# Windowed attention and softplus feed-forward: a new hand-written opening that reaches slot 9

## The chip, the cores and the metric

One NeuronCore of a Trainium2 chip runs the whole program. The metric is the time of one execution on the device in microseconds. Before the change the median of three runs is 897.19 us (895.76 to 897.30).

## The reference

```python
def _attn_ref(q, k, v):                       # q, k, v: (8, 8, 576, 64)
    scores = scale * np.matmul(q, k.transpose(0, 1, 3, 2))
    mask_plain = (rel >= 0) & (rel < 32)
    mask_dil = (rel >= 0) & (rel < 128) & (rel % 4 == 0)
    masks = ...                               # plain for heads 0 to 3, dilated for 4 to 7
    scores = np.where(masks, scores, -1e9)
    attn = softmax(scores)                    # sum + 1e-9 under the exponentials
    return np.matmul(attn, v)

x = attn_out.transpose(0, 2, 1, 3).reshape(4608, 512)
h = x @ w_in                                  # (512, 2048)
g = np.maximum(h, 0) + np.log1p(np.exp(-np.abs(h)))
return g @ w_out                              # (2048, 512)
```

## The kernel before

The 4608 tokens are cut into nine chunks of 512. A chunk has four attention groups of two heads each (groups 0 to 3 are chunk 0, 4 to 7 are chunk 1, and so on); the first two groups of a chunk have the plain window, the last two the dilated one. Only keys in the window are multiplied, in blocks of 32 queries by 64 keys. The feed-forward has 16 slices of 128 hidden columns (ff). Every product is made of three matrix products, from a high and a low part of each factor: high by high, high by low, low by high.

The first two chunks run through 32 *slots*, one for a chunk and a slice each, listed by `RUNS`: slots 0 to 5 are slices 0 to 5 of chunk 0, slots 6 to 15 slices 0 to 9 of chunk 1, slots 16 to 25 the rest of chunk 0, slots 26 to 31 the rest of chunk 1. Slot i has four H parts (`h_part(i, kt)`, line 545: hidden columns from the 128 input columns kt, which are those of attention group kt of the chunk) and four O parts (`o_part(i, m)`, line 610: output columns m). O of slot i - 2 follows H of slot i. An O part adds into its output bank over the slots of a run; at the last slot of the run the four banks are copied to SBUF and sent to DRAM (`kept_part`, line 637), to be added when the chunk resumes.

Weights arrive as 64-bit words and are decoded on the chip, one tensor (ff, 0 for w_in or 1 for w_out) in seven steps (`decode_step`, line 141): D0 absolute value (ScalarE), D1 to D4 clamp, shift and merge (VectorE), D5 the high part (ScalarE), Dl the low part (VectorE, or GpSimd for the first five).

All of the work up to a certain place is written out by hand in the string `OPENING` (line 71). Each word is one step; the instructions of an engine run in the order of the words. The words are: k, q, v, m, r loads of keys, queries, values, masks and raw weights (r0, r1, ... in the order in which slots need them: (0,0), (1,0), (0,1), (2,0), (1,1), (3,0), ...); S the scores of a group, M their maximum, E the exponentials (16 rows on ScalarE), Z the divisor, P the division (GpSimd; Pv on VectorE), T four transposes on TensorE, C the copy of their result (ScalarE; Cv on VectorE), V the product with the values, Xh and Xl the high and low part of its result; H and O the parts of a slot; A the three activation rows on ScalarE, G the softplus sum, Gh and Gl its high and low part; F that many filler products on zeros, whose result is not read. The list before ends with O of slot 4 (`OPENED = 6`); from slot 7 on a loop (line 917) writes H and O parts in turn and puts the other work between them by planned times.

PSUM is laid out by tags: "h" with two banks for hidden columns, "att" with two banks, "o0" to "o3" for the output parts. Scores of odd groups of chunk 0 use the two h banks, all other scores use att. Transposes use o0 and value products o1 and o2 for chunk 0, and att for every later group:

```python
self.turned_to = two_banks("t_ps", ("o0",) if self.own else None)[0][0]    # transposes, own: chunk 0
banks, src = two_banks("a_ps", ("o1", "o2") if self.own else None)         # weighted
```

Of the kernel before, what the change touches and what calls it, by code (L numbers as in the profile page):

```python
# [39 lines left out]
NKT = DM // P  # L40
NPR = H // 2
NFF = DF // P
RUNS = ((0, 6), (1, 10), (0, 10), (1, 6))
OPENED = 6
FIRST = 2
HALF = CH // 2
NPAIR = NFF // 2
# [4 lines left out]
LAG = 2  # L52
# [16 lines left out]


OPENING = """
k0 q0 m0 k1 q1 v0 F8 S0 q2 M0 k2 F1 S1 q3 E0 M1 r0 k3 E1 F7 S2 Z0 P0 r1 M2 F2 T0 v1 D0_0_0 Z1 S3
P1 E2 C0 v3 V0 M3 r2 T1 D1_0_0 Xh0 D2_0_0 E3 v2 C1 Xl0 m1 D3_0_0 F5 V1 r3 Z2 D4_0_0 Xh1 P2 k5 Xl1
D0_0_1 q4 Z3 F6 T2 D5_0_0 P3 k4 D0_1_0 q5 C2 D1_1_0 D1_0_1 v4 F4 V2 D2_0_1 D3_0_1 T3 k6 Xh2 D4_0_1
S4 C3 Xl2 Dl0_0 r4 D5_0_1 Dl0_1 M4 F1 H0_0 D0_2_0 r5 V3 D2_1_0 E4 D3_1_0 H0_1 r6 D4_1_0 H0_2 Xh3
D1_2_0 Xl3 v5 D2_2_0 F3 H0_3 D5_1_0 D3_2_0 S5 q6 A0 Z4 Dl1_0 r7 M5 P4 H1_0 D0_3_0 H1_1 G0 r8 E5
H1_2 Gh0 Gl0 H1_3 k7 D1_3_0 D2_3_0 D3_3_0 r9 A1 F3 T4 Z5 D4_2_0 D4_3_0 r10 G1 P5 C4 D5_2_0 F7 V4
r11 D0_1_1 Gh1 Gl1 D5_3_0 D1_1_1 Xh4 v6 Dl3_0 Xl4 Dl2_0 D0_3_1 q7 F7 T5 r12 D2_1_1 D0_2_1 H2_0
D3_1_1 C5 H2_1 D4_1_1 r13 H2_2 D1_2_1 D5_1_1 V5 D2_2_1 D3_2_1 r14 D4_2_1 H2_3 Xh5 D1_3_1 O0_0
D5_2_1 Xl5 Dl1_1 A2 O0_1 v7 S7 Dl2_1 r15 D2_3_1 D0_4_0 O0_2 G2 D0_5_0 O0_3 M7 r16 H3_0 D1_4_0 H3_1  # L80
E7 D2_4_0 r17 H3_2 D3_4_0 H3_3 D4_4_0 O1_0 Gh2 r18 Gl2 D5_4_0 O1_1 Z7 A3 S6 Dl4_0 r19 D1_5_0 O1_2
D2_5_0 D0_4_1 M6 P7 O1_3 r20 H4_0 G3 E6 H4_1 D3_5_0 r21 H4_2 D4_5_0 H4_3 D3_3_1 O2_0 r22 D5_5_0
Gh3 T7 Z6 A4 Dl5_0 O2_1 Gl3 r23 O2_2 D4_3_1 O2_3 C7 G4 P6 H5_0 r24 D5_3_1 H5_1 D0_6_0 Gh4 V7 Gl4
r25 Dl3_1 H5_2 Xh7 D1_4_1 H5_3 D0_5_1 Xl7 r26 O3_0 A5 D2_4_1 T6 D3_4_1 O3_1 r27 D4_4_1 O3_2 C6
D1_6_0 G5 O3_3 r28 D5_4_1 Gh5 V6 Gl5 Dl4_1 H6_0 Xh6 r29 D1_5_1 H6_1 D0_7_0 Xl6 D2_5_1 H6_2 r30
D2_6_0 H6_3 D3_6_0 O4_0 D4_6_0 A6 r31 O4_1 D3_5_1 O4_2 D4_5_1 D5_6_0 O4_3 D1_7_0 G6 D5_5_1 Gh6 Gl6
Dl5_1 Dl6_0 D2_7_0 D3_7_0 D4_7_0 D5_7_0 Dl7_0
"""


# [1 line left out]
def tile_windowed_attention_softplus_ffn(  # L92
# [201 lines left out]
    class Group:  # L294
# [7 lines left out]
        def __init__(self, c, pr):  # L302
            self.c, self.pr, self.dil = c, pr, pr >= NPR // 2
            self.own, self.masked = c == 0, c < 2

        def load_k(self, engine=None):
            kw = DKW if self.dil else PKW
# [92 lines left out]
            ))  # L400

        def transposes(self):
            self.turned_to = two_banks("t_ps", ("o0",) if self.own else None)[0][0]
            for m in range(NS):
                tc.keep_in_program_order(
                    nc.tensor.transpose(
                        out=self.turned_to[:, m * P : (m + 1) * P],
                        in_=self.s[:, m * P : (m + 1) * P],
                        identity=ident,
                    )  # L410
                )
            self.pt = scratch([P, CH], "pt", self.c, self.pr)
# [36 lines left out]

        def weighted(self):  # L450

            banks, src = two_banks("a_ps", ("o1", "o2") if self.own else None)
            for i in range(NB):
                t2, g = divmod(i, NG)
                for h in range(2):
                    for r in range(2):
                        rows = slice(r * D, (r + 1) * D)
                        if self.dil:
                            at = g * (PER // 2) + t2 * BLK
                            dst = banks[h][rows, at : at + BLK]  # L460
                        else:
                            by_class = banks[h][rows, :HALF].rearrange("p (r i) -> p r i", r=DIL)
                            dst = by_class[:, :, i * BLK // DIL : (i + 1) * BLK // DIL]
                        matmul(
                            out=dst,
                            lhsT=self.v[h * WKEYS : (h + 1) * WKEYS, i, r, :],
                            rhs=self.weights_of(h, r * 2 + t2, g),
                            start=True,
                            stop=True,
                        )  # L470
            if self.c >= FIRST:
                self.x = x_half(self.c, self.pr // 2)[:, self.pr % 2], None, src
# [50 lines left out]
    def at(when, part, *what, cost=0.0):  # L523
        heapq.heappush(events, (when, next(serial), cost, part, what))
# [128 lines left out]
    def fillers(n):  # L653
# [523 lines left out]
```

## Time and profile before

| | before |
|---|---|
| median of 3 runs | 897.19 us |
| the profiled execution | 896.0 us |
| its span, first to last instruction | 893.9 us |
| TensorE busy | 873.5 us, 98% |
| VectorE busy | 607.5 us, 68% |
| ScalarE busy | 551.2 us, 62% |
| GpSimd busy | 49.0 us, 5% |
| granted TensorE clock, mean | 0.99 |

Busy shares are means over the whole span. The page cuts the span in 40 slices of 22.3 us: TensorE is busy 6, 9 and 8 tenths of the first three, the granted clock is 8 tenths in the first two, and GpSimd works in the first three alone. In the chain that ended last TensorE has 89% of the span, VectorE 4%, ScalarE 3%, DMA and its queue 2%. Times in the views count from the start of the span.

### The profile page before, as it was taken

To read this page: it belongs to the slowest core of one execution; us is meant where nothing else is said; L and a number is where in the kernel's file an instruction comes from. 1 tells how busy PE (TensorE), PEld (TensorE's weight loads), DVE (VectorE), ACT (ScalarE), POOL (GpSimd) and SP (SyncE) were. 2 spreads that over 40 slices of the span, in tenths; PEclk is the share of its full clock that TensorE was granted. 3 is DMA by queue.
4 is the path that set the end of the run, shared out by engine and by line. 5 is a ranking of instruction groups with operands and counts; after the bars stand their busy time and mean duration, and the time that the engine had idled before them with its cause. 6 is when DMAs were issued, how large, how long until landed. Compare 5 with 4: busy or idle time off the path is not lost.

```text
span 893.9 us, 22746 instructions
## 1 busy us (share of the span) xinstructions
PE 873.5 (98%) x9186; PEld 747.8 (84%) x9186; DVE 607.5 (68%) x1216; ACT 551.2 (62%) x1355; POOL 49.0 (5%) x47
## 2 busy tenths in 40 slices
PE   6989899999999999999999999999999999999998
PEld 3668678888888888888888888888888888899997
DVE  2799889898678667655765666667666766565544
ACT  4676687766756566556665565557555765455443
POOL 1320000000000000000000000000000000000000
PEclk8899999999999999999999999999999999999999
DMA  9778222764465456554555455544654564334333
GB/s 345 285 256 330 73 75 74 273 234 147 156 208 172 151 157 209 173 166 148 196 191 167 145 178 206 163 156 165 194 171 159 160 204 135 106 106 154 95 95 118
DMA packets 84296, 154.12 MB, mean 172 GB/s; under 512 B 9312, under 2 KB 25824, under 8 KB 84192
## 3 DMA queue, kind: packets, MB, share of 16 engines
q1 hardware_dynamic: 83472, 151.49, 50.4%
q8 instruction: 73, 1.20, 0.6%
q10 hardware_dynamic: 720, 1.18, 0.4%
q14 instruction: 31, 0.25, 0.1%
HBM read 125.37 MB, written 27.26 MB: 171 GB/s over the span
## 4 chain that ended last, share of the span: by engine, by line
PE 89%; DVE 4%; ACT 3%; issue 1%; DMA 1%; SPq 1%; ACTq 0%; DVEq 0%
PE o_ps L182 42%; PE h_x L182 18%; PE h_y L182 14%; PE h_ps L182 7%; PE a_ps L182 4%; PE s_ps L182 3%; ACT s L377 1%; DVE a L166 1%; DMA k<-kpl 1%; DVE a L161 1%; DVE parts L176 1%; SPq L131 1%; ACT ob L638 0%; ACT parts L173 0%; DVE e L567 0%
## 5 line engine op out<-in xcount | busy, mean ns | idle before, releaser
L182 PE MATMUL o_ps<-gh,t 128*128 128x512 f32 (+1 forms) x904 | 341.2, 391 | 0.0
L182 PEld LDWEIGHTS o_ps<-gh,t 128*128 128x128 f32 x904 | 169.8, 188 | 21.3
L560 ACT ACTIVATE e<-hs 128x512 f32<-128x512 f32 x112 | 70.3, 627 | 188.0 <-DVE hs L956 188.0
L182 PE MATMUL o_ps<-gl,t 128*128 128x512 f32 (+1 forms) x452 | 178.4, 395 | 0.0
L582 ACT CAST gh<-e 128x512 fp32r<-128x512 f32 x137 | 84.6, 618 | 64.3 <-DVE e L567 63.4
L588 DVE TENSOR_TENSOR gl<-e,gh 128x512 fp32r<-128x512 f32 x144 | 104.2, 724 | 10.8 <-ACT gh L582 9.5
L182 PEld LDWEIGHTS h_x<-a,parts 128*128 128x128 f32 x672 | 95.2, 189 | 9.8 <-DVE hs L956 0.3
L182 PEld LDWEIGHTS h_y<-s,t 128*128 128x128 f32 x672 | 93.9, 188 | 9.0
L182 PE MATMUL h_y<-s,t 128*128 128x256 f32 x672 | 99.6, 284 | 0.0
L182 PE MATMUL h_x<-a,parts 128*128 128x256 f32 x672 | 98.1, 282 | 0.0
L562 ACT ACTIVATE e<-e 128x512 f32<-128x512 f32 x144 | 91.2, 633 | 4.6
L561 ACT ACTIVATE e<-e 128x512 f32<-128x512 f32 x144 | 91.1, 633 | 4.6
L956 DVE TENSOR_TENSOR hs<-h_x,temps 128x256 f32<-128x256 f32 x112 | 47.4, 423 | 66.2 <-PE h_x L182 64.8
L182 PE MATMUL o_ps<-gh,parts 128*128 128x512 f32 x256 | 88.9, 399 | 3.5 <-ACT ob L638 3.5
L956 DVE TENSOR_TENSOR temps<-h_y,temps 128x256 f32<-128x256 f32 x112 | 47.5, 424 | 61.2 <-PE h_y L182 61.1
L182 PEld LDWEIGHTS o_ps<-gl,t 128*128 128x128 f32 x452 | 86.4, 191 | 3.1 <-DVE gl L588 0.4
L182 PE MATMUL h_ps<-xh,parts 128*128 128x512 f32 x256 | 87.9, 399 | 0.0
L395 POOL TENSOR_TENSOR s<-s,ri 128x512 f32<-128x512 f32 x36 | 41.4, 1149 | 685.7 <-DVE ri L392 485.3
L567 DVE SCALAR_TENSOR_TENSOR e<-hs,e 128x512 f32<-128x512 f32 x112 | 76.3, 681 | 1.8 <-ACT e L562 1.8
L377 ACT ACTIVATE s<-s,nm 128x64 f32<-128x64 f32 x224 | 74.8, 336 | 3.9 <-DVE nm L369 3.9
L182 PEld LDWEIGHTS o_ps<-gh,parts 128*128 128x128 f32 x256 | 48.7, 190 | 14.1 <-ACT ob L638 3.9
L182 PEld LDWEIGHTS h_ps<-xh,parts 128*128 128x128 f32 x256 | 48.6, 190 | 10.4
(80 smaller groups left out, 1223.1 us busy)
## 6 DMA issues: line engine op xcount, KB each, us to landing
t<-w_out SPq DMA_DIRECT2D x224, 256.0 KB, 3.0
v<-vp SPq DMA_DIRECT2D x36, 512.0 KB, 4.1
raw<-w SPq DMA_DIRECT2D x32, 512.0 KB, 9.0
q<-qp SPq DMA_DIRECT2D x36, 256.0 KB, 3.2
w_out<-parts SPq DMA_DIRECT2D x16, 512.0 KB, 4.7
out_t<-ob SPq DMA_DIRECT2D x32, 256.0 KB, 2.3
turned<-squares SPq DMA_DIRECT2D x28, 256.0 KB, 3.6
pt<-turned SPq DMA_DIRECT2D x112, 64.0 KB, 2.8
```

The lines of the kernel that those rows point to most:

```text
L131: tc.keep_in_program_order((engine or nc.sync).dma_start(**kw))
L161: pin(nc.vector.scalar_tensor_tensor(out=ai, in0=low, scalar=29, in1=ai, op0=ALU.logical_shift_right, op1=ALU.bitwise_or,))
L182: tc.keep_in_program_order(nc.tensor.matmul(**kw))
L377: pin(nc.scalar.activation(out=self.blocks[:, t], in_=src, func=AF.Exp, bias=self.nm[:, t : t + 1], scale=1.0 / 8.0 if self.masked else 1. ...
L395: pin((engine or nc.gpsimd).tensor_tensor(out=self.blocks, in0=self.blocks, in1=self.ri.unsqueeze(2).to_broadcast([P, NB, WKEYS]), op=ALU. ...
L560: pin(nc.scalar.activation(out=e, in_=tiles[i], func=AF.Abs))
L561: pin(nc.scalar.activation(out=e, in_=e, func=AF.Exp, scale=-1.0))
L562: pin(nc.scalar.activation(out=e, in_=e, func=AF.Ln, bias=1.0))
L567: pin(nc.vector.scalar_tensor_tensor(out=e, in0=tiles.pop(i), scalar=0.0, in1=e, op0=ALU.max, op1=ALU.add))
L582: pin(nc.scalar.copy(out=gh, in_=ready[i]))
L588: pin(nc.vector.tensor_tensor(out=gl, in0=e, in1=gh.bitcast(F32), op=ALU.subtract))
L956: pin(nc.vector.tensor_tensor(out=dst, in0=src, in1=temps[:, temp], op=ALU.add))
```

## The change

It rewrites `OPENING`, which now goes on to O of slot 7 (`OPENED = 9`), and moves the start of chunk 2's attention in the planned part from 9 to 10.2 slots. Groups 4 and 5 get the banks o0 (transposes) and o1, o2 (value products) that chunk 0's groups have, through `AHEAD = 6`. An output bank is taken by its own O part and no longer by part 0 for all four. The four copies after slot 5 are words of the list (K). The high part of g is on VectorE for slots 0 to 9, but for slot 4 (Gs, ScalarE); after slot 9 it is on ScalarE. One division (Pv4) and two copies (Cv4, Cv7) are on VectorE. There are 38 fillers in place of 54.

```diff
-OPENED = 6
+OPENED = 9
+AHEAD = 6
 OPENING = """
-k0 q0 m0 k1 q1 v0 F8 S0 q2 M0 k2 F1 S1 q3 E0 M1 r0 k3 E1 F7 S2 Z0 P0 r1 M2 F2 T0 v1 D0_0_0 Z1 S3
...
+k0 q0 m0 k1 q1 q2 v0 F9 S0 k2 M0 r0 E0 F3 S1 r1 M1 k3 Z0 E1 q3 F5 S2 P0 v1 M2 T0 k4 D0_0_0 Z1 v2 C0
...
@@ class Group
             self.own, self.masked = c == 0, c < 2
+            self.ahead = c * NPR + pr < AHEAD
...
-            self.turned_to = two_banks("t_ps", ("o0",) if self.own else None)[0][0]
+            self.turned_to = two_banks("t_ps", ("o0",) if self.ahead else None)[0][0]
...
-            banks, src = two_banks("a_ps", ("o1", "o2") if self.own else None)
+            banks, src = two_banks("a_ps", ("o1", "o2") if self.ahead else None)
...
-    def g_high(i):
+    def g_high(i, copy=None):
         gh = g_tile("h", i)
-        if i <= OPENED:
-            pin(nc.vector.tensor_copy(out=gh, in_=ready[i]))
-        else:
-            pin(nc.scalar.copy(out=gh, in_=ready[i]))
+        pin((copy or nc.scalar.copy)(out=gh, in_=ready[i]))
         ready[i] = ready[i], gh
...
-    obs = {}
+    obs, keeping = {}, {}
...
+        if first:
+            o_ps[m] = bank(f"o_ps{m}", f"o{m}")
         if m == 0:
-            if first:
-                for k in range(NKT):
-                    o_ps[k] = bank(f"o_ps{k}", f"o{k}")
             if final and not resumed:
                 ob_tiles(c)
...
+        elif final and i + LAG <= OPENED:
+            keeping[m] = c, o_ps[m]
         elif final:
             at(now[0] + 0.12, kept_part, m, c, o_ps[m])
...
-        "Gh": g_high,
+        "Gh": lambda i: g_high(i, nc.vector.tensor_copy),
+        "Gs": g_high,
+        "K": lambda m: kept_part(m, *keeping.pop(m)),
...
-        attend(FIRST * NPR + j, 9 + 3.6 * j, 3.5)
+        attend(FIRST * NPR + j, 10.2 + 3.5 * j, 3.5)
```

What the list makes of three places follows, as rows of an engine's order (line, operation, output<-inputs, shape of the output).

ScalarE near the start, before: the exponentials of groups 0 and 1 (two pairs of rows for the odd one), then the Abs of the first raw weight, the exponentials of group 2, the copy C0 of group 0's turned weights and xh of group 0.

```order
L377 ACTIVATE s_189,sm_198<-s_ps_142,nm_190 128x64 x4
L377 ACTIVATE s_189,sm_198<-s_ps_143,nm_190 128x64 x4
L150 ACTIVATE a_271<-raw_194 128x512
L377 ACTIVATE s_256,sm_313<-s_ps_215,nm_257 128x64 x8
L441 COPY pt_268<-t_ps_263 128x512
L490 CAST xh_359<-a_ps_325 128x256
```

The same place now:

```order
L381 ACTIVATE s_194,sm_204<-s_ps_156,nm_195 128x64 x4
L381 ACTIVATE s_194,sm_204<-s_ps_157,nm_195 128x64 x4
L153 ACTIVATE a_271<-raw_141 128x512
L445 COPY pt_268<-t_ps_263 128x512
L381 ACTIVATE s_259,sm_281<-s_ps_221,nm_260 128x64 x8
L494 CAST xh_328<-a_ps_294 128x256
```

The copy C0 has changed places with the exponentials of group 2.

TensorE at the transposes and value products of groups 4 and 5, before: the end of H1, T4, V4, T5, the start of H2 (seven fillers stand in each of the two gaps next to V4).

```order
L182 MATMUL h_ps<-xh,parts 128x512
...
L406 MATMUL t_ps<-ident,s 128x128 x4
...
L182 MATMUL a_ps<-pt,v 64x4x8 x32
...
L406 MATMUL t_ps<-ident,s 128x128 x4
L182 MATMUL h_ps<-xh,parts 128x512
```

The same groups now, from H1_0 to the product after T5: T4, H1_1 to H0_3, V4, the scores of group 6, H1_3, two fillers, T5.

```order
L410 MATMUL t_ps<-ident,s 128x128 x4
L185 MATMUL h_ps<-xh,parts 128x512
...
L185 MATMUL a_ps<-pt,v 64x4x8 x32
L185 MATMUL s_ps<-k,q 32x64 x32
...
L185 MATMUL h_ps<-xh,parts 128x512
...
L410 MATMUL t_ps<-ident,s 128x128 x4
```

H parts and the scores of group 6 stand between the steps of groups 4 and 5, where fillers stood.

ScalarE at the copies of the output banks after slot 5, before: the activation of slot 8 (h_ps_1386), three copies, two decode rows, the fourth copy.

```order
L560 ACTIVATE e_1411<-h_ps_1386 128x512
L561 ACTIVATE e_1411<-e_1411 128x512
L562 ACTIVATE e_1411<-e_1411 128x512
L638 COPY ob_1417<-o_ps0_928 128x512
L638 COPY ob_1417<-o_ps1_929 128x512
L638 COPY ob_1418<-o_ps2_930 128x512
L173 CAST parts_1437<-a_1392 128x512
L150 ACTIVATE a_1439<-raw_1022 128x512
L638 COPY ob_1418<-o_ps3_931 128x512
```

Now: the activation of slot 7 (h_ps_1350), the four copies, one Abs, the activation of slot 8 (h_ps_1398).

```order
L564 ACTIVATE e_1375<-h_ps_1350 128x512
L565 ACTIVATE e_1375<-e_1375 128x512
L566 ACTIVATE e_1375<-e_1375 128x512
L640 COPY ob_1370<-o_ps0_1006 128x512
L640 COPY ob_1370<-o_ps1_1014 128x512
L640 COPY ob_1371<-o_ps2_1021 128x512
L640 COPY ob_1371<-o_ps3_1034 128x512
L153 ACTIVATE a_1417<-raw_999 128x512
L564 ACTIVATE e_1427<-h_ps_1398 128x512
```

The copies have moved from behind the activation of slot 8 to ahead of it.

## Rows read from the trace of the kernel before

**Rows 1.** Busy time by stretch: from:to, length, engines (rows), PEclk, DMA, GB/s.
```profile
20.00:25.00 5.00, 3.60 (x12) 1.72 (x11) 1.94 (x6) 3.20 (x18) 1.25 (x1) 0.50 1.05 404
...
100.00:105.00 5.00, 5.00 (x76) 3.60 (x75) 2.97 (x6) 4.20 (x9) 0.00 (x0) 0.66 0.56 210
...
110.00:180.00 70.00, 69.08 (x658) 56.11 (x657) 59.33 (x109) 56.30 (x137) 3.62 (x3) 1.00 0.41 140
...
300.00:890.00 590.00, 590.00 (x5966) 522.48 (x5965) 370.64 (x758) 346.02 (x809) 22.82 (x20) 1.00 0.49 158
```

**Rows 2.** Order of time, TensorE: first product of slots 10 and 11 (start, length).
```profile
110.25 0.39 PE L182 MATMUL h_ps<-xh,parts 128*128 128x512 f32 x1
...
115.69 0.39 PE L182 MATMUL h_ps<-xh,parts 128*128 128x512 f32 x1
```

**Rows 3.** Order of time, TensorE: scores and what follows, transposes, value product.
```profile
30.96 0.86 PE L182 MATMUL s_ps<-k,q 64*32 64x64 f32 x64
...
31.98 0.38 PE L182 MATMUL unread<-still 128*128 128x512 bf16 x1
...
78.10 0.60 PE L406 MATMUL t_ps<-ident,s 128*128 128x128 f32 x4
...
80.69 1.13 PE L182 MATMUL a_ps<-pt,v 64*64 64x32 f32 x64
```

**Rows 4.** Groups of TensorE by form, 0 to 100 us: the fillers (busy, mean ns).
```profile
L182 PE MATMUL unread<-still 128*128 128x512 bf16 x54 | 17.2, 457 | 1.3 <-POOL still L214 1.3
```

**Rows 5.** Order of time, 11 to 32 us, ScalarE, VectorE and TensorE.
```profile
11.36 0.31 ACT L377 ACTIVATE s<-s_ps,nm 128x64 f32<-128x64 f32 x1 [1.76 <-DVE sm L389]
...
13.60 0.24 ACT L377 ACTIVATION_READ_ACCUMULATOR s<-s_ps,nm 128x1 f32 x1
13.69 0.71 ACT L150 ACTIVATE a<-raw 128x512 f32<-128x512 f32 x1
...
17.23 0.62 ACT L441 COPY pt<-t_ps 128x512 f32<-128x512 f32 x1
...
17.91 1.30 PE L182 MATMUL a_ps<-pt,v 64*64 64x32 f32 x61 [1.42 <-ACT pt L441]
...
21.33 0.42 PE L182 MATMUL a_ps<-pt,v 64*64 64x32 f32 x3 [2.12 <-issue]
...
22.20 0.42 DVE L494 TENSOR_TENSOR xl<-a_ps,xh 128x256 fp32r<-128x256 f32 x1 [2.12 <-ACT xh L490]
...
22.54 0.68 DVE L161 SCALAR_TENSOR_TENSOR a<-raw,a 128x512 int32<-128x512 int32 x1
...
32.01 0.58 PE L182 MATMUL h_ps<-xh,parts 128*128 128x512 f32 x1
```

**Rows 6.** Order of time, TensorE: T4, T5 and the last product of H2.
```profile
45.72 0.63 PE L406 MATMUL t_ps<-ident,s 128*128 128x128 f32 x4 [0.47 <-issue]
...
52.48 0.63 PE L406 MATMUL t_ps<-ident,s 128*128 128x128 f32 x4 [1.77 <-DVE xl L494]
...
56.74 0.40 PE L182 MATMUL h_ps<-xh,parts 128*128 128x512 f32 x1
```

**Rows 7.** Order of time, TensorE: the last product of H8, the first of O6.
```profile
95.51 0.39 PE L182 MATMUL h_ps<-xh,parts 128*128 128x512 f32 x1
...
99.37 0.50 PE L182 MATMUL o_ps<-gh,parts 128*128 128x512 f32 x1 [3.48 <-ACT ob L638]
```

**Rows 8.** Order of time: a GpSimd row, a VectorE step beside it, the step alone.
```profile
29.17 1.46 POOL L176 TENSOR_TENSOR parts<-a,parts 128x512 fp32r<-128x512 f32 x1
29.42 1.50 DVE L152 TENSOR_SCALAR a<-a 128x512 f32<-128x512 f32 x1
...
36.60 0.42 DVE L152 TENSOR_SCALAR a<-a 128x512 f32<-128x512 f32 x1
```

**Rows 9.** Waits of TensorE, 0 to 110 us: total, times, longest.
```profile
PE a_ps L182 <- issue: 3.7, 3, 2.1
```

**Rows 10.** Order of time, TensorE: five fillers between 20 and 25 us.
```profile
22.59 2.34 PE L182 MATMUL unread<-still 128*128 128x512 bf16 x5
```

More of the change, by code (lines that the diff above doesn't have):

```diff
@@ L71 @@
 OPENING = """
-k0 q0 m0 k1 q1 v0 F8 S0 q2 M0 k2 F1 S1 q3 E0 M1 r0 k3 E1 F7 S2 Z0 P0 r1 M2 F2 T0 v1 D0_0_0 Z1 S3
[L73 to L87, printed above, removed]
+k0 q0 m0 k1 q1 q2 v0 F9 S0 k2 M0 r0 E0 F3 S1 r1 M1 k3 Z0 E1 q3 F5 S2 P0 v1 M2 T0 k4 D0_0_0 Z1 v2 C0
@@ new lines @@
+D1_0_0 D2_0_0 E2 F3 V0 D3_0_0 r2 D4_0_0 S3 Xh0 P1 v3 Xl0 F1 T1 D0_1_0 M3 r3 D5_0_0 Z2 C1 Dl0_0 q4 E3
+F4 V1 k5 D1_1_0 m1 D2_1_0 q5 D3_1_0 Xh1 r4 D4_1_0 Xl1 P2 D0_0_1 F5 H0_0 r5 D5_1_0 Z3 H0_1 D1_0_1
+D0_2_0 T2 D2_0_1 k6 D3_0_1 S4 C2 v4 D1_2_0 D4_0_1 V2 M4 P3 q6 D5_0_1 r6 Xh2 D2_2_0 F1 T3 D3_2_0 E4
+r7 Xl2 Dl0_1 C3 F3 H0_2 k7 D4_2_0 V3 Dl1_0 r8 D0_3_0 Z4 S5 D5_2_0 Pv4 r9 Xh3 D1_3_0 H1_0 D0_1_1 M5
+Dl2_0 v5 T4 H1_1 Xl3 E5 H1_2 q7 Cv4 r10 H0_3 D2_3_0 D3_3_0 V4 A0 Z5 r11 D1_1_1 S6 D2_1_1 D3_1_1 v6
@@ new lines @@
+Xh4 H1_3 M6 P5 D0_2_1 r12 Xl4 E6 F2 T5 G0 r13 Gh0 F2 H2_0 C5 Gl0 H2_1 r14 D4_1_1 V5 A1 Z6 D4_3_0 r15
+S7 D1_2_1 D2_2_1 Xh5 v7 G1 P6 H2_2 D5_3_0 Xl5 H2_3 D5_1_1 r16 Dl3_0 M7 O0_0 A2 O0_1 Dl1_1 r17 O0_2
+E7 O0_3 G2 r18 H3_0 Gh1 Gl1 H3_1 r19 Gh2 H3_2 D0_4_0 Gl2 T6 D0_3_1 r20 Z7 H3_3 D3_2_1 C6 O1_0 D4_2_1
+A3 r21 V6 D1_4_0 D2_4_0 r22 D3_4_0 O1_1 Xh6 D4_4_0 O1_2 D5_2_1 r23 Xl6 P7 O1_3 D5_4_0 G3 Dl2_1 r24
+T7 Cv7 r25 D0_5_0 Dl4_0 V7 D1_5_0 D0_4_1 D2_5_0 r26 H4_0 Xh7 D3_5_0 H4_1 D4_5_0 r27 H4_2 Xl7 D5_5_0
@@ new lines @@
+H4_3 Gh3 r28 O2_0 Dl5_0 A4 O2_1 Gl3 r29 O2_2 D1_3_1 D2_3_1 D0_6_0 O2_3 D3_3_1 r30 H5_0 D4_3_1 H5_1
+G4 D5_3_1 r31 H5_2 D1_4_1 Gs4 H5_3 Dl3_1 Gl4 A5 O3_0 D2_4_1 O3_1 D3_4_1 O3_2 D4_4_1 D0_5_1 O3_3 G5
+D5_4_1 H6_0 D1_5_1 H6_1 Dl4_1 H6_2 D2_5_1 D0_7_0 D3_5_1 H6_3 D4_5_1 O4_0 A6 Gh5 O4_1 Gl5 O4_2 D1_7_0
+D5_5_1 O4_3 D2_7_0 D3_7_0 H7_0 Dl5_1 H7_1 D4_7_0 H7_2 G6 D5_7_0 H7_3 Gh6 O5_0 A7 Dl7_0 O5_1 Gl6 O5_2
+D1_6_0 D2_6_0 K0 O5_3 G7 K1 H8_0 Gh7 K2 H8_1 Gl7 K3 H8_2 D3_6_0 D0_7_1 H8_3 D4_6_0 O6_0 A8 D1_7_1
@@ L88 @@
+O6_1 D2_7_1 O6_2 D3_7_1 D5_6_0 O6_3 G8 H9_0 Gh8 Gl8 H9_1 Dl6_0 H9_2 D4_7_1 H9_3 O7_0 D5_7_1 A9 O7_1
+O7_2 Dl7_1 O7_3 G9 Gh9 Gl9
 """
```

## The prediction

> **What bounds the kernel.** I read the busy time by stretch first, then the order of time on TensorE, and then on the engines that it waits for in the opening. From 110 us on TensorE hardly ever stops: 69.1 of 70 us, and from 300 to 890 every microsecond [rows 1]. Slot 10's first product starts at 110.25 and slot 11's at 115.69 [rows 2], so a slot of eight parts (four H, four O) takes 5.44 us and a part 0.68. The time of this kernel is therefore the moment at which TensorE has finished a given place in its order, plus work that the change leaves alone. I take the start of H10_0, 110.25, as that place, because the new list ends just ahead of it.
>
> Ahead of it stand 40 H parts and 32 O parts (72 x 0.68 = 49.0) and eight attention groups. A group's score takes 1.0 (30.96 to 31.98), its transposes 0.6 and its value product 1.1 [rows 3]: 2.7, eight times 21.6. The score of group 8 (1.0) is also ahead in the old order and behind in the new one, so I take it off. 110.25 - 1.0 - 70.6 leaves 38.6 us that were **lost** to waits, fillers (54, 17.2 us busy [rows 4]) and a slow clock. A change of the opening can move only these. By stretch:
> - to H0_0 at 32.01 [rows 5]: five scores, four transposes, three value products are 10.8; lost 21.2.
> - on to the end of H2 at 57.1 [rows 6]: 12 parts, one score, two transposes, three value products are 13.7 of 25.1; lost 11.4.
> - on to the end of H8 at 95.9 [rows 7]: 48 parts and the last two groups are 38.0 of 38.8; lost 0.8.
> - on to H10_0: 12 parts and the score are 9.2 of 14.35; lost 5.1.
>
> **The last stretch: the copies out of the output banks.** After slot 5 ScalarE copies four banks, but in the old list's loop these copies stand behind slot 8's activation, and all four banks are taken at O6_0. TensorE waits 3.48 us for them [rows 7]; the clock granted in 100 to 105 is 0.66 [rows 1], which stretches O6. In the new order the copies stand ahead of slot 8's activation, beside H8 on TensorE, and each bank is taken by its own part. Four copies are 2.5 us, at the 0.62 of the bank copied at 17.23 [rows 5]; H8 is 2.7 and covers them, and if they came late, O6_0 would wait for one copy, not for four and an activation. Gain 5.1, the surest term; between 3.5 (only the wait goes) and 5.1.
>
> **The first stretch: H0_0 earlier.** Here the raw load is not what is late. The first weight's Abs runs at 13.69, but its third decode step stands behind the second half of xl of group 0 and runs at 22.54, right after it (22.20) [rows 5]. That half waited for V0, which started at 17.91 and stopped 2.12 us for nothing but issue [rows 5]. V0 in turn waited for the copy of the turned weights at 17.23, queued behind E2. So putting the raw weight one 256 KB load earlier is worth nothing by itself; the order on ScalarE and VectorE is worth something. In the new order the copy stands ahead of E2: E1 ends at 13.84, the Abs at 14.4, the copy at 15.0, and V0 can run from 15.1 to 16.2. VectorE does all four steps of the weight ahead of xl, done near 17.7. Then ScalarE has E2 to 17.6 (16 rows take 13.84 - 11.36 = 2.5), then xh, the next Abs and the high part of the first weight (0.6 to 0.7 each) to 19.6 and the copy for group 1 to 20.2. GpSimd's low part (1.46) is there at 21.2; V1 runs 20.3 to 21.5; five fillers follow; H0_0 starts at **23.0**. To there TensorE has four scores, two transposes, two value products: 7.5. Lost 15.5 instead of 21.2.
>
> **The second stretch, to the end of H2.** Old: groups 4 and 5 share one pair of banks ("att") with every score, so T4 (45.72) comes only behind E5, which reads its scores there, and T5 (52.48) for xl of group 4: 1.77 idle, behind fourteen fillers [rows 6]. New: their transposes go to o0 and their sums to o1 and o2, and E5, S6, T5, V5, S7 no longer queue behind each other. TensorE's content is 12 parts 8.2, four scores 4.1, four transposes 2.4, four value products 4.4 and eight fillers 1.7: 20.8. Three waits come on top. H0_1 needs xl of group 1, which stands behind the second weight on VectorE: 1.4. H0_2 needs xl of group 2: VectorE has 5.8 us of rows between the two, and three GpSimd operations fall among them; a step of 0.42 took 1.50 beside one of 1.46 [rows 8], so I charge 3.4 more; TensorE has 4.7 us for these 9.2, so it waits 4.5. V5 needs the copy of group 5, behind E6: 1.1. The end of H2 is 23.0 + 20.8 + 7.0 = **50.8**, lost 8.7 instead of 11.4.
>
> **The third stretch gives some back.** Groups 6 and 7 stay in att and now come close together: T6 waits until E7 has read att (0.7), T7 for xl of group 6 (1.0), and V7 stands right behind T7 with nothing between, so it waits for the copy, which VectorE now makes (1.4). What queues behind it is all of H4. Lost 0.8 + 3.1. From H4 on I find no wait: each low part and each decoded weight ends up to five us ahead of its product.
>
> **Other edits, at no cost here.** Sixteen fillers go; they stood in waits. The division of group 4 and two copies move to VectorE, three high parts of g too, and xl of groups 4 and 5 is two pieces: each 0.2 to 0.7 us, in the queues walked above. After slot 10 VectorE is about two weights behind where it was (a weight is five rows, 2.9 us); it was idle 10.7 of the 70 us from 110 on [rows 1], which hides it; without that cover up to 5.8 would come back.
>
> **The sum.** Gain (21.2 - 15.5) + (11.4 - 8.7) - 3.1 + 5.1 = 10.4. The profiled execution took 896.0: 885.6. The median of the three runs is 1.2 above it, so I say **886**. The bounds of what I can't see: "issue" stops cost the value products 3.7 us in the old order [rows 9] and may fall on the new chain in full (gain 6.7), or GpSimd may block less than charged (below). The forecast's own range is 883 to 890.
>
> **Rivals.**
> - **GpSimd costs nothing.** If VectorE slips its rows in between, the 3.4 goes and the later stalls shrink by 1.8: gain 15.6, 881. For: the operations may fall where VectorE waits anyway. Against: rows 8, where a row waits out the whole of one. Chance 0.20.
> - **The array runs at half clock.** [...] The new order has 38 fillers, and a wait of 4.5 after H0_0. If H0_2 to H1_3 (eight parts or their equal, some 5 us) run at that level, they cost 5 more: gain 5.4, 891. For: rows 1 and 10. Against: 54 fillers did not prevent it either. Chance 0.15. [...]
> - **The start does not move.** If V0 or V1 stops for issue again and the loads arrive as they did, H0_0 stays near 30 and only the banks and the copies gain: about 4, 892. Chance 0.10.
> - **Slower.** H4 waits for V7, and V7 for a copy at the end of VectorE's queue of Z7, six decode steps, xl, softplus and a low part, with ScalarE's E7, C6, A3 ahead of those. I walk H4_0 to 65.4 (50.8, twelve parts of O0, H3 and O1, two transposes, two value products, 3.1 of waits), with 10.4 in hand, so the change loses once H4_0 starts after 75.8: one wait of over ten microseconds. Fifteen of them, some 900. Against: VectorE has no wait of that size in the old trace. Chance 0.05.
>
> **How the numbers follow.** The forecast has 0.46, the rivals 0.20, 0.15, 0.10, 0.05; 0.04 is left for no change. A measurement of this kernel tells about 0.2%, 1.8 us. Everything up to 895.4 counts as faster: 0.90; same 0.04; slower 0.06. The range reaches down past the first rival and up past the third: 880 to 893, with the slower case, no change and the tails of the others left out.
>
> **What would show it.** Right: H0_0 near 23, H2 done near 51, H4_0 near 65, H10_0 near 99; no wait of O6 for the copies; T5 not released by xl of group 4; 38 fillers. Wrong in a term: H0_0 after 27 (first stretch), H2 after 55 (second), a granted clock below 0.9 between 25 and 50 (clock rival), a long wait at V7. Wrong as a whole: H10_0 after 107, or new waits on TensorE between 110 and 180.

## The result, and the profile after

The changed kernel takes 901.41 us (median of 5, 899.73 to 902.96), the kernel before 897.19 (5 runs, 895.76 to 897.50): a ratio of 1.0048, 95% interval 1.0031 to 1.0066. Forecast were 886 and a gain; it is slower, by half a percent, and outside the range.

| | forecast | after |
|---|---|---|
| H0_0 starts | 23.0 | 26.54 |
| H2 ends | 50.8 | 57.31 |
| H4_0 starts | 65.4 | 70.29 |
| H10_0 starts (before: 109.25 without group 8's score) | 99 | 103.08 |
| H10_0 to the end of slot 31's O (before: 145.7) | 146.7 | 158.4 |
| profiled execution, span | 885.6 | 901.4, 899.4 |
| TensorE busy; mean granted clock | | 97%; 0.988 |

So the new list did gain on the way to H10_0, 6.2 of the 10.4 us forecast, and 11.7 were lost behind the place at which the forecast stopped looking. (146.7 is the 145.7 of before and the score of group 8, 1.0, which now stands behind H10_0.) From the end of slot 31's output on both kernels take 638 us.

In all views PE is TensorE, PEld its weight loads, DVE VectorE, ACT ScalarE and POOL GpSimd; "issue" is time in which an engine waited for nothing that the profile shows.

Stretches of [rows 1], the half-clock stretch of the opening and the change of loops (where the second loop of the program begins), in the profile after:

```profile
20.00:25.00 5.00, 3.79 (x41) 2.24 (x44) 2.86 (x8) 1.57 (x9) 1.11 (x1) 0.66 1.04 399
...
45.00:50.00 5.00, 3.72 (x12) 2.35 (x13) 2.98 (x7) 2.30 (x16) 0.00 (x0) 0.50 0.89 263
...
100.00:105.00 5.00, 5.00 (x68) 3.95 (x69) 3.04 (x6) 3.50 (x6) 0.00 (x0) 1.00 0.00 0
...
110.00:180.00 70.00, 65.12 (x636) 52.98 (x635) 56.65 (x105) 54.38 (x141) 3.85 (x3) 0.98 0.39 137
...
242.00:262.00 20.00, 16.54 (x185) 13.74 (x183) 14.64 (x32) 10.55 (x23) 0.00 (x0) 0.83 0.62 188
```

100 to 105 is mended: full clock (1.00), no wait. From 45 to 50 the granted clock is 0.50, the lower of the two values that it has in this trace (1.00 and 0.50); it was 1.00 there before. And 110 to 180 had 69.1 us of TensorE in [rows 1] and has 65.1 now, and 242 to 262, full before (20.00 of 20 at 1.00), has 16.5 at a clock of 0.83. The waits of TensorE by what they wait for (total, times, longest), first 0 to 110 us, then 110 to 300:

```profile
PE s_ps L185 <- issue: 6.4, 3, 4.0
PE a_ps L185 <- issue: 2.1, 1, 2.1
PE unread L185 <- issue: 1.8, 1, 1.8
PE h_ps L185 <- DVE xl L498: 1.7, 1, 1.7
...
PE a_ps L185 <- DVE pt L445: 1.1, 1, 1.1
...
PE s_ps L185 <- ACT x_full L494: 4.7, 3, 2.3
PE h_y L185 <- DVE e L571: 2.8, 1, 2.8
PE o_ps L185 <- DVE gl L589: 0.7, 1, 0.7
```

Two readings. In the opening TensorE stops 10.3 us for nothing but issue; before, a_ps had 3.7 of that [rows 9], s_ps and t_ps 0.5 each. Behind slot 10 there are 8.2 us of waits where the old kernel had one of 0.8. The stops for issue in order of time, TensorE (start, length, and in brackets the stop ahead of it), with the first product of H0_0:

```profile
15.03 0.38 PE L185 MATMUL unread<-still 128*128 128x512 bf16 x1 [1.76 <-issue]
15.34 1.14 PE L185 MATMUL a_ps<-pt,v 64*64 64x32 f32 x64
16.40 0.84 PE L185 MATMUL s_ps<-k,q 64*32 64x64 f32 x62
21.21 0.37 PE L185 MATMUL s_ps<-k,q 64*32 64x64 f32 x2 [3.96 <-issue]
...
26.54 0.58 PE L185 MATMUL h_ps<-xh,parts 128*128 128x512 f32 x1
...
42.85 1.13 PE L185 MATMUL a_ps<-pt,v 64*64 64x32 f32 x63 [2.06 <-issue]
43.91 0.97 PE L185 MATMUL s_ps<-k,q 64*32 64x64 f32 x64
46.28 0.61 PE L185 MATMUL s_ps<-mask,consts 128*128 128x256 bf16 x2 [1.39 <-issue]
...
55.17 0.42 PE L185 MATMUL s_ps<-k,q 64*32 64x64 f32 x21 [1.03 <-issue]
```

V0 and S3 (the second and third row) stand back to back, and S3 stops after 62 of its 64 pairs; a pair is a weight load and a product. The maximum, the exponentials of group 3 (to 26.4) and H0_0, which takes their banks, all follow the last two. V4 with S6 and V5 with S7 are neighbours too.

Behind slot 10: TensorE and ScalarE around the score of group 9, TensorE at that of group 11, then VectorE and TensorE where the second loop begins:

```profile
124.58 1.14 PE L185 MATMUL a_ps<-pt,v 64*64 64x32 f32 x64
...
125.73 0.62 ACT L176 CAST parts<-a 128x512 fp32r<-128x512 f32 x1 [0.40 <-DVE a L169]
126.26 0.67 ACT L153 ACTIVATE a<-raw 128x512 f32<-128x512 f32 x1
126.83 0.56 ACT L494 COPY x_full<-a_ps 128x512 f32<-128x512 f32 x1
127.45 0.86 PE L185 MATMUL s_ps<-k,q 64*32 64x64 f32 x64 [1.73 <-ACT x_full L494]
...
173.30 0.86 PE L185 MATMUL s_ps<-k,q 64*32 64x64 f32 x64 [2.30 <-ACT x_full L494]
...
243.25 1.28 DVE L715 TENSOR_TENSOR b<-parts 128x512 f32<-128x512 f32 x2
...
246.16 0.68 DVE L571 SCALAR_TENSOR_TENSOR e<-h_ps,e 128x512 f32<-128x512 f32 x1
...
246.91 1.65 PE L185 MATMUL h_y<-s,t 128*128 128x256 f32 x6 [2.79 <-DVE e L571]
```

The score of group 9 follows the value product of group 8 directly and shares its banks, so it waits for the copy out of them, and ScalarE has two decode rows ahead of that copy, one waiting for VectorE. At 246 the last softplus of slot 31 stands behind sums of weights (L715 and its followers) that came earlier in the old order. Six products that take 0.98 in e3 and e5 take 1.65 here, at a granted clock of 0.50 (246.0 to 252.6).

### The profile page after: what moved, and what is told of

It reads as the page before. It is cut to its first block, busy times and chain, and to the rows that moved or that the text cites. A ratio compares the mean times of both kernels' runs of the same rounds, so it can differ in the third digit from the quotient of the medians.

```text
span 899.4 us, 22716 instructions
## 1 busy us (share of the span) xinstructions
PE 871.6 (97%) x9170; PEld 748.6 (83%) x9170; DVE 610.8 (68%) x1223; ACT 548.7 (61%) x1353; POOL 48.0 (5%) x46
## 3 DMA queue, kind: packets, MB, share of 16 engines
q8 instruction: 72, 1.18, 0.5%
q10 hardware_dynamic: 720, 1.18, 0.4%
## 4 chain that ended last, share of the span: by engine, by line
PE 83%; DVE 7%; ACT 5%; issue 2%; DMA 1%; POOL 0%; SPq 0%; DVEq 0%; ACTq 0%; POOLq 0%
PE o_ps L185 39%; PE h_x L185 18%; PE h_y L185 14%; PE h_ps L185 5%; PE a_ps L185 4%; PE s_ps L185 3%; ACT s L381 2%; DVE gl L589 1%; DVE e L571 1%; PE unread L185 1%; DVE a L164 1%; DVE a L169 1%; ACT e L565 1%; ACT gh L583 1%; ACT e L564 0%
```

## The experiments

Theories: **blocks** (TensorE's instructions are late in the opening), **neighbours** (3.5 slots between groups put a value product and a score that shares its banks side by side), **debt**, later **order** (decode pieces left over from the shorter opening stand ahead of what TensorE needs). In the table, "start" is H10_0's, "between" the time from there to the end of slot 31's O, "waits" those of TensorE from 110 to 300 us, all from the one profiled execution; those of e1, e2 and e8 were the shortest of theirs (893.2, 892.7 and 905.8). The seven profiles with this opening unchanged up to slot 6 (after, e1, e2, e3, e6, e8, e12) have H0_0 at 26.5 to 29.0, and slot 10, e8 left out, at 101.0 to 105.2, so a single start says little below 4 us. e1 to e4, e5 to e8 and e9 to e12 were each run on one chip beside the kernel before, whose medians there were 896.54, 896.18 and 896.00; across these groups the ratios compare better than the medians.

| run | median us | ratio to before (95%) | start | between | waits |
|---|---|---|---|---|---|
| before | 897.19 | | 110.25 | 145.7 | 0.8 |
| after | 901.41 | 1.0048 (1.0031 to 1.0066) | 103.1 | 158.4 | 8.2 |
| e1 spacing | 896.39 | 1.0004 (0.9994 to 1.0013) | 101.2 | 152.2 | 4.9 |
| e2 debt | 896.55 | 1.0002 (0.9991 to 1.0013) | 101.0 | 151.8 | 6.0 |
| e3 both | 897.11 | 1.0001 (0.9992 to 1.0009) | 104.7 | 152.6 | 5.2 |
| e4 old, close | 899.14 | 1.0031 (1.0021 to 1.0042) | 109.8 | 149.3 | 3.8 |
| e5 fewer fillers | 892.83 | 0.9962 (0.9949 to 0.9974) | 100.7 | 152.3 | 4.8 |
| e6 slack | 896.80 | 1.0005 (0.9995 to 1.0014) | 105.2 | 152.9 | 5.2 |
| e7 slack, fillers | 893.56 | 0.9973 (0.9963 to 0.9983) | 101.2 | 152.9 | 5.1 |
| e8 copies late | 907.56 | 1.0122 (1.0109 to 1.0136) | 108.2 | 157.6 | 7.9 |
| e9 one weight more | 891.78 | 0.9950 (0.9936 to 0.9963) | 102.8 | 149.9 | 3.8 |
| e10 fillers again | 891.75 | 0.9952 (0.9940 to 0.9964) | 99.5 | 152.3 | 4.8 |
| e11 both again | 891.25 | 0.9940 (0.9924 to 0.9956) | 100.3 | 149.9 | 3.9 |
| e12 loaded transfers | 896.83 | 1.0004 (0.9994 to 1.0014) | 104.5 | 152.3 | 4.9 |

**e1, the spacing alone.**
```diff
-        attend(FIRST * NPR + j, 10.2 + 3.5 * j, 3.5)
+        attend(FIRST * NPR + j, 10.2 + 3.6 * j, 3.5)
```


> The changed kernel with one number put back: chunk 2's attention groups again 3.6 slots apart (10.2 + 3.6j), no longer 3.5, so that one part stands between a value product and the next score. Theory 'neighbours': at 3.5 the value product of group n and the score of group n+1 stand next to each other on TensorE, and the score waits for ScalarE's copy of the value product out of the same banks. Then the waits 's_ps <- ACT x_full' between 110 and 300 us (4.7 us in three) fall under 1.5, the slow clock near 175 goes, slot 22 starts some 4 us earlier, and the time is 896.5 to 898.5 (from 901.4); the wait of 2.8 at the change of loops stays. Rival 'late VectorE': the copy is late since ScalarE stands behind decoding that is behind in any case; then the waits only move to another place, slot 22 starts where it did, and the time is within 1 us of 901.4.

5.0 us faster by the medians, 3.9 by the ratios. The waits of 110 to 300 now (with 0.6 more for a low part of g):

```profile
PE h_y L185 <- DVE e L571: 2.8, 1, 2.8
PE s_ps L185 <- ACT x_full L494: 1.5, 2, 0.8
```

The copy's share is down from 4.7 to 1.5, the edge of what "neighbours" has, and the clock in 173 to 180 is 1.00.

**e2, the debt alone.**
```diff
-        behind += pump(time) - 0.69
+        behind += pump(time) - 0.72
```


> The changed kernel with the planner's allowance of VectorE work per part raised from 0.69 to 0.72 us, so that the decoding and weight-sum pieces that wait in its list (109 at slot 10 against 97 before the change) are all out before slot 31 ends; in the changed kernel three are left and fall in ahead of the last softplus. Theory 'debt': the wait of 2.8 of the second loop's first product for the last softplus, and the half clock at 248 to 253 that follows it, vanish; in 242 to 262 TensorE is busy over 19 of 20 us and the time is 895 to 897. The waits for x_full stay. Rival 'another cause': that wait comes from the softplus' own inputs or from ScalarE; then it stays above 2 us, and the time is within 1 us of 901.4, or above it, where more VectorE work per part makes the low parts of g late.

4.9 us faster by the medians, 4.1 by the ratios, TensorE busy 20.00 of 20 in 242 to 262, and the waits:

```profile
PE s_ps L185 <- ACT x_full L494: 4.7, 3, 1.6
PE o_ps L185 <- DVE gl L589: 0.8, 1, 0.8
PE h_y L185 <- DVE e L571: 0.5, 1, 0.5
```

Each edit removes the wait that its theory names. Whether they are two losses or one is the question of the next run.

**e3, both edits.**

> Both: 3.6 slots between the groups and 0.72 us per part. If 'neighbours' and 'debt' are two separate losses, their gains add: 4 and 5.5, so 890.5 to 893, below both kernels, with slot 31's O done near 251 to 252 and TensorE busy over 131 of the 132 us from 110 to 242. If they are one loss (the later one appears because the earlier one shifted the work), both gains together are that of the larger alone, about 895.5 to 897.

No more than either alone, near the expectation's second case, one loss. Other waits stand in place of the two:

```profile
PE s_ps L185 <- ACT x_full L494: 1.8, 3, 0.9
PE o_ps L185 <- DVE sm L393: 1.2, 1, 1.2
PE o_ps L185 <- ACT ob L640: 0.9, 1, 0.9
PE o_ps L185 <- DVE gl L589: 0.8, 1, 0.8
PE h_y L185 <- DVE e L571: 0.5, 1, 0.5
```

Part of the loss could go only once. Of the 11.7 us lost behind slot 10, 7.4 are the waits above those of before, which leaves 4.3; the granted clock after the two longest waits is low (0.76 in 173 to 180, 0.66 in 244 to 254), which I take for most of these 4.3. By the table this rest is 1.4 in e1 and nothing in e2, so either edit wins most of it. Why e1's remaining wait of 2.8 cost less clock (0.81 in 236 to 242, around it, and 0.94 in the ten us behind) was not settled.

**e4, the kernel before with its groups 3.5 apart** (`9 + 3.5 * j` for `9 + 3.6 * j`).

> The kernel before the change with its groups 3.5 slots apart (9 + 3.5j for 9 + 3.6j), nothing else. 'Neighbours' expects waits 's_ps <- ACT x_full' of 3 to 6 us between 100 and 200 in place of 0.8, and a time of 899.5 to 903 (from 897.2). If the copies are late only because the new opening leaves VectorE behind, the old kernel, which has more of its decoding done, shows under 1.5 us of such waits and 897 within 1.

2.6 us slower by the medians of the same chip (896.54), 0.3% by the ratio, with 3.8 us of waits for x_full in place of 0.8. The spacing hurts the old kernel too, somewhat under the size expected; it isn't the new opening's lag that makes the copy late.

**e5, twelve fillers fewer ahead of S3**, on e1.
```diff
-k0 q0 m0 k1 q1 q2 v0 F9 S0 k2 M0 r0 E0 F3 S1 r1 M1 k3 Z0 E1 q3 F5 S2 P0 ...
+k0 q0 m0 k1 q1 q2 v0 F3 S0 k2 M0 r0 E0 F1 S1 r1 M1 k3 Z0 E1 q3 F1 S2 P0 ...
```


> As the run with the spacing put back, and twelve of the twenty filler products ahead of group 3's score left out (9, 3, 5 become 3, 1, 1; each is two instructions, a weight load and a product, so 24 instructions). Theory 'blocks': TensorE's instructions arrive in packets of 16,384 bytes, and it stops where a packet's instructions are used up before the next has landed. In all four profiles of this opening so far it stopped at the same instructions: after 62 of the 64 pairs of S3, after the first pair of V4, just ahead of the mask products of S6, after 43 pairs of S7; between S6's stop and S7's stand 252 instructions. With 24 fewer ahead, every stop lies 24 instructions further on: S3 runs through, the stop of up to 4.0 us falls behind it (by T1 or V1), V4 stops after 13 pairs or so, S6 does not stop. Since E3 and H0_0 wait for S3's end, H0_0 starts at 22.5 to 25 (from 26.6), and the time is 1 to 4 us under that run's 896.4, unless the later queue of VectorE takes it back. Rival 'saturated transfers': the stop comes whenever the loads fill the DMA engines, at 17 to 21 us, whichever instruction stands there; then S3 still stops for 2 us or more, or S6 still stops, and the time stays at 896.4 within 1. Rival 'fillers matter': fewer of them halve the granted clock in 10 to 30 us below 0.7, and the time rises.

3.6 us under e1 by the medians, 3.8 by the ratios. The stops of its opening over 0.4 us from 20 us on (start, and the stop ahead of it):

```profile
21.15 0.38 PE L185 MATMUL unread<-still 128*128 128x512 bf16 x1 [2.67 <-issue]
...
39.34 1.00 PE L185 MATMUL a_ps<-pt,v 64*64 64x32 f32 x51 [0.43 <-issue]
50.14 0.44 PE L185 MATMUL s_ps<-k,q 64*32 64x64 f32 x9 [2.81 <-issue]
```

S3 runs through, V4 stops with 51 pairs left (after 13), S6 not at all, S7 with 9 left (after 55): each stop lies 24 instructions further on, to the pair. H0_0 starts at 24.50. S7's stop has grown, though, and took most of it back before slot 10 in this profile. So e5's profile is only 0.3 us under that of e1, the shortest of its 11 runs; the gain of the medians shows in the profiles of e6 and e7 below. These twelve fillers fewer lowered no clock: 1.00 in 10 to 20, 0.83 in 20 to 30, in e1 the same.

**e6, slack in place of a larger allowance**, on e1 (`behind + early[0][1] < 0.8` for `< 0.4`), and **e7, the same on e5**.

> Spacing 3.6, and in place of a larger allowance of VectorE work per part (0.72, which did not add to the spacing's gain) the old one of 0.69 with a later limit: a waiting piece may go in while the planner's lag is under 0.8 instead of 0.4 us. All pieces are out by slot 31, as with 0.72. If the two losses are separate and 0.72 only made other VectorE steps late (the 0.9 and 1.2 us waits of o_ps for the copies of slot 16 and near 220 us), the waits of TensorE from 110 to 262 fall from 5 to 3 us or less, and the time is 893.5 to 895. If VectorE's lag is one loss that shows at whichever place has the least slack, the waits still sum to 4 to 6 us, and the time is 896 to 897.5.

> The two runs before this in one: spacing 3.6, limit 0.8, twelve fillers fewer ahead of S3. 'Blocks' with a separate VectorE loss: 890 to 893, under both kernels. If VectorE sets the moment at which the second loop can begin, whatever the opening does, the earlier H0_0 is given back between 110 and 262 in new waits, and the time is within 1 us of the run without the fillers' change.

Neither beats its base (896.39, 892.83); the waits sum to 5.2 and 5.1 at other places, which is what e6 was to show if VectorE's lag is one loss that comes out wherever there is least slack. So "neighbours" and "debt" are not two losses that add: with either edit or both, "between" stays at 151.8 to 152.9. The 3.2 us between e6 and e7, medians of one chip, are the fillers': slot 10 starts at 105.2 and 101.2, and "between" is 152.9 in both, so the opening's gain is not lost behind slot 10. (893.56 is just above the 890 to 893 of "blocks".)

**e8, the copies late again**, on the changed kernel.
```diff
-... K0 O5_3 G7 K1 H8_0 Gh7 K2 H8_1 Gl7 K3 H8_2 D3_6_0 D0_7_1 H8_3 D4_6_0 O6_0 A8 ...
+... O5_3 G7 H8_0 Gh7 H8_1 Gl7 H8_2 D3_6_0 D0_7_1 H8_3 D4_6_0 A8 K0 K1 K2 K3 O6_0 ...
-        if first:
-            o_ps[m] = bank(f"o_ps{m}", f"o{m}")
         if m == 0:
+            if first:
+                for k in range(NKT):
+                    o_ps[k] = bank(f"o_ps{k}", f"o{k}")
```


> The changed kernel with its third part alone undone: the four copies out of the output banks stand behind slot 8's activation again, and slot 6's first output part takes all four banks. My forecast put 5.1 us on this part (3.5 at least). On the way there: TensorE waits about 3.5 us for the copies at O6_0 near 95, the clock drops after it, and slot 10 starts 4 to 5 us later, near 107.5. At the end: if the opening's gains are lost behind slot 10 to a VectorE that is behind, the later start costs less than that, since VectorE catches up meanwhile: 901.5 to 903.5; if gains add, 905 to 906.5.

6.2 us slower by the medians, 6.6 by the ratios, above both ranges expected; slot 10 starts at 108.24. TensorE at O6_0, and its waits behind slot 10:

```profile
98.29 0.50 PE L185 MATMUL o_ps<-gh,parts 128*128 128x512 f32 x1 [2.48 <-ACT ob L641]
...
PE s_ps L185 <- ACT x_full L494: 4.5, 3, 2.3
PE h_y L185 <- DVE e L571: 2.8, 1, 2.8
```

O6_0 waits 2.5 us, not the 3.5 expected, and from the end of H8 to H10_0 it is 12.4 us in place of 8.0; the rest of the later start is this profile's opening, with H0_0 at 29.0. VectorE had 5 us more to slot 10, and the waits behind it are the same to 0.3 us. So "VectorE catches up" is wrong: its order is fixed, and a piece that stands ahead of a softplus held it back whatever time there was earlier (TensorE's wait for that softplus is 2.8 in the profile after and 2.8 here).

**e9, one weight more in the list**, on e5: the steps D0 to D5 and Dl of (6,1) among the words of slots 8 and 9.
```diff
-... D4_6_0 O6_0 A8 D1_7_1 ... H9_1 Dl6_0 H9_2 D4_7_1 H9_3 O7_0 D5_7_1 A9 O7_1 ... Gl9
+... D4_6_0 O6_0 A8 D0_6_1 D1_7_1 ... H9_1 Dl6_0 D1_6_1 H9_2 D4_7_1 D2_6_1 H9_3 O7_0 D5_7_1 D3_6_1 A9 O7_1 ... Gl9 Dl6_1
```


> As the run with spacing 3.6 and twelve fillers fewer (892.8), and one weight more, (6,1), decoded by words of the list in slots 8 and 9, where VectorE is idle some 2 us in 95 to 105, so that the planner has five pieces fewer behind slot 10 and none is left over at slot 31. In all runs so far, also in the one that came 5 us later to slot 10, the stretch from H10_0 to the end of slot 31's output took 5 to 6 us more than before the change (12 with the two losses of the changed kernel), so the loss sits in the planned order and not in VectorE's time. Theory 'order': with five pieces out of that order, the second loop's first product waits under 1 us in place of 2.8, the stretch from H10_0 shrinks by 1.5 to 3, and the time is 889.5 to 891.5. Rival 'same loss elsewhere': the waits of TensorE from 110 to 262 stay at 4.5 to 6 us in sum at other places, or the low parts of g wait behind the new steps in slots 8 to 10, and the time is 892 to 894.

"Between" shrinks from 152.3 to 149.9 and the wait at the second loop from 2.8 to 0.5, so the pieces left in the planned order were the cause of that wait. The waits for x_full grow from 1.5 to 2.5, and 3.2 us above 146.7 are left. The median falls by 1.1 to 891.78, just above the range expected; the intervals of e5 and e9 overlap.

**e10, thirteen more fillers out** between S3 and S7, and **e11, e9 and e10 in one**.

> As the run with spacing 3.6 and twelve fillers fewer (892.8), and thirteen more fillers left out between S3 and S7 (26 instructions). There S7 stopped 2.8 us nine pairs before its end. 'Blocks': it now ends without a stop, V4 stops after some 26 pairs, and the stop of S7 falls among the parts of H2, shorter by the time that the instructions ahead of it take, so slot 10 starts 0.5 to 2 us earlier (100.7 there) and the time is 891 to 892.8. Rival 'fillers matter': the granted clock of 20 to 55 us falls below 0.85 (0.90 there), and the time is over 893.5.

> The two runs before this in one. If the opening's gain and the order behind slot 10 are separate, their gains add: 888 to 891. If the first part's gain is lost behind slot 10, it is within 0.5 of the run with one weight more alone.

In e10 S7 ends without a stop and slot 10 starts at 99.5. V4's stop, expected after some 26 pairs, does not show there; in e11, with the same words ahead of it, it comes after 23. That of S7 comes among the parts of H2, as long as before, not shorter:

```profile
51.57 0.50 PE L185 MATMUL h_ps<-xl,parts 128*128 128x512 f32 x1 [2.72 <-issue]
```

The clock in 20 to 55 is 0.81 in e10, below the 0.85 that was the sign of "fillers matter", but the time is not over 893.5, and in e11, with the same fillers out, the clock is 0.92 there. So these profiles do not show that fillers hold the clock up. e11, 891.25, beats both kernels: 0.9940 (0.9924 to 0.9956). e9, e10 and e11 can't be told apart by their intervals, so whether the last two gains add is open.

**e12, useless transfers beside V4 and S6**, on e1: two copies of 1 MB in DRAM, on ScalarE's queue (`J0 J1` behind `D5_2_0`).

> The kernel with the spacing put back alone, and two transfers of 1 MB from one place of DRAM to another, issued on ScalarE's queue at 35 to 36 us, of no use to the result. At 34 to 43 us the DMA engines were nearly idle there, and the packets with TensorE's instructions started 3.4 to 3.7 us apart around V4 and S6, against 6.1 where the loads fill the engines. Theory 'one packet after another, each slower under load': V4's and S6's stops (1.0 to 2.1 and 1.4 to 1.8 us) stay at the same instructions and sum to 5 to 8 us, packets 5 to 6.5 us apart. Rival 'a stop has a fixed length': they sum to 2.4 to 3.9 as before.

TensorE at V4 and S6, then the busy times from 39 to 46 us (columns as above; the last two are the DMA engines' busy share and GB/s), of e12:

```profile
42.88 1.13 PE L185 MATMUL a_ps<-pt,v 64*64 64x32 f32 x63 [1.53 <-issue]
...
48.77 0.61 PE L185 MATMUL s_ps<-mask,consts 128*128 128x256 bf16 x2 [3.97 <-issue]
...
39.00:46.00 7.00, 4.27 (x139) 3.30 (x137) 5.12 (x12) 5.43 (x22) 1.05 (x1) 0.95 1.03 406
```

and of e1:

```profile
41.44 1.13 PE L185 MATMUL a_ps<-pt,v 64*64 64x32 f32 x63 [0.97 <-issue]
...
44.86 0.39 PE L185 MATMUL s_ps<-mask,consts 128*128 128x256 bf16 x2 [1.50 <-issue]
...
39.00:46.00 7.00, 4.53 (x139) 3.40 (x137) 4.97 (x10) 4.92 (x20) 1.05 (x1) 0.94 0.45 155
```

The two stops fall at the same instructions and sum to 5.5 in place of 2.5; the two packets with TensorE's instructions start 6.05 us apart in place of 3.44. V4's stop (1.5) lies within the 0.2 to 2.1 of the other profiles with this opening; it is S6's, 4.0 against 1.4 to 1.8, that the load lengthened. So the order of instructions says where TensorE stops, and the load on the DMA engines, as far as one profile shows, how long.

## Why the prediction was wrong

By stretch, in the terms of the sum, the gains were 2.2, -0.3, -1.0 and 5.3 us where 5.7, 2.7, -3.1 and 5.1 were forecast. Nearly all of the 6.2 up to H10_0 is the copies, and all of that and more was lost behind slot 10, where the sum had nothing. (885.6 and 1.2 make 886.8, not 886; nothing hangs on it.)

- **The copies** ("the surest term", 5.1): right. They run at 91.5 to 93.5 beside the end of O5 and H8, O6_0 follows H8 with no wait, and from the end of H8 to H10_0 it is 8.0 us; before, it was 13.4 without the score. Undoing them costs 6.2 (e8), 4.4 of it in this stretch. The copies, the last product of H8 and the first of O6:

```profile
91.51 2.03 ACT L640 COPY ob<-o_ps 128x512 f32<-128x512 f32 x4
...
94.69 0.39 PE L185 MATMUL h_ps<-xh,parts 128*128 128x512 f32 x1
...
94.92 0.39 PE L185 MATMUL o_ps<-gh,parts 128*128 128x512 f32 x1
```

- **The first stretch** (H0_0 at 23.0): the order argued for ScalarE and VectorE came true; V0 ran at 15.34 (forecast 15.1 to 16.2), though its copy was done at 14.0, with a stop for issue of 1.8 ahead of V0, and the first weight was decoded ahead of xl. What failed is "the bounds of what I can't see": stops for issue were kept as an edge of the range, 3.7 us at most, and not put in the sum. S3's stop alone is 4.0, more than the whole difference to 26.54. Moved by 24 instructions (e5) it frees H0_0 to 24.5; in e10 H0_0 starts at 22.2, in e11 at 24.3.
- **The second stretch** (H2 ends 27.8 after H0_0): 30.8. I charged 7.0 of waits for xl and the copy, 3.4 of it to GpSimd; it is 1.7 at H0_2. That the charge was too high by 5.3 is the size of the first rival, but by luck: 1.4 and 1.1 of it are the waits at H0_1 and V5, which did not come, and GpSimd did cost something, as a VectorE step of 0.69 shows beside two GpSimd rows:

```profile
31.75 3.15 POOL L179 TENSOR_TENSOR parts<-a,parts 128x512 fp32r<-128x512 f32 x2 [2.73 <-ACT parts L176]
32.14 1.64 DVE L164 SCALAR_TENSOR_TENSOR a<-raw,a 128x512 int32<-128x512 int32 x1
```

  The charge was hidden by stops of 2.1, 1.4 and 1.0 that stand nowhere in the sum, and by some 4 us of slower clock (0.50 in 45 to 50) and short waits.
- **The third stretch** (3.1 given back before H4): about 1.4; 1.1 of it is V7 waiting for its copy. The rival that ended slower needed a wait of over ten us there; H4_0 started at 70.29, ahead of the limit of 75.8. The kernel did get slower, but not by that mechanism.
- **Behind slot 10** ("it was idle 10.7 of the 70 us from 110 on, which hides it"): wrong, and this turned the sign. Two weights behind were seen; three are (the planner's list held 109 pieces at slot 10, before 97, and has four for a weight). But VectorE's idle time, 13.4 of the same 70 us in the profile after, did not hide it: its order is fixed, and the late pieces stood where it had none to spare (busy 6.86 of 7 us in 120 to 127, 7.86 of 8 in 165 to 173, 3.90 of 4 in 242 to 246). "Without that cover up to 5.8" was a bound on VectorE's time; 11.7 were lost: 7.4 of waits, since late pieces stood ahead of what TensorE needed, and 4.3 that I take for the low clock behind the two longest. The prediction's own sign of being wrong as a whole, new waits between 110 and 180, is what came. With either edit or both some 5 us stay lost, with e9 3.2; what would remove these is open.
- **The spacing** of 3.5 for 3.6 slots stands in the diff and nowhere in my sum: the step that was left out altogether. It costs the old kernel 2.6 (e4), and putting it back gives the new one 5.0 (e1; 3.9 by the ratios).
- **The half-clock rival** came true in part, and not where it was priced: the clock of 20 to 25 rose from 0.50 to 0.66, and the parts from 32 to 40 ran at full level (1.00), but behind the stops at V4 and S6 it fell to 0.50 in 45 to 50 (1.00 before), so that 25 to 50 has 0.89, under the 0.9 that was its sign. It was low again behind 173 and 246 (0.76 in 173 to 180, 0.66 in 244 to 254), where I did not look. What half the clock costs shows in five fillers: 2.34 before, at 0.50 [rows 10], and 1.25 from 25.64 on in the profile after, at 1.00.

## What to carry to other kernels

Stopping a sum at a place "behind which nothing changes" needs that place's queues, not only its time: compare what each engine's fixed order still holds there, and every planner number that the diff touches behind it. Where attention products of many small instructions stand side by side, count instructions: here a value product and a score with its mask products are 260, where a packet has 255 on average, and 252 of them ran in 1.9 us; a filler is two. An engine's idle share need not hide a late step (VectorE's 13.4 of 70 us did not); look at the slack of the step right behind it. And where one order of instructions starts a place at 101 in one profile and at 105 in another, compare medians and several profiles before a gain of that size is called shown.

## What the runs showed of the hardware

The page of the changed kernel counts 72 packets of kind instruction on queue q8, 1.18 MB, each 16,384 bytes in the trace. I take them for TensorE's instructions: its 9170 weight loads and 9170 products make 255 for a packet, and the stops lie about as far apart. Between those at V4, S6 and S7 stand 254 and 252 instructions (a weight load and a product for each pair), and moving 24 moved the stops at S3, V4 and S7 by 24 (V4 and S7 at the same pairs in e5, e7 and e9). While the loads fill the DMA engines (busy 1.03 to 1.04 of each stretch between two packets in e5), packets start 6.0 to 6.1 us apart (12.63, 18.69, 24.83, 30.83, 36.89 in e5); with the engines less busy 3.4 (e1, around V4 and S6) to 3.7 (in the profile after, 40.22 and 43.89, the engines 0.06 busy in between). V0 and the 62 pairs of S3, 252 instructions, run from 15.34 to 17.24, in 1.9. What sets the moment at which a packet is asked for stays open: in the profile after, the one nearest to S3's stop started 1.5 us after TensorE had stopped, that at V4 0.6 us before.

The opening also varies from run to run: e1 and e12 have the same words but for two transfers and start slot 10 at 101.2 and 104.5, and e1 alone spans 893.2 to 898.4 in 11 runs, where the kernel before spans 895.1 to 898.1 in 31.
